# Attention with unsplit exponentials and values: plain fp32 value products on two 64-column halves of the array, and a new queue order

## The chip, the core and the metric

The kernel runs on one core of a Trainium2 chip. The core has five engines with a queue each, which run on their own and wait for one another by semaphores: PE (TensorE, matmuls from SBUF into PSUM), DVE (VectorE), ACT (ScalarE), POOL (GpSimd) and SP (which issues the DMAs). The metric is the time of one execution in microseconds, median of several runs.

## What is computed

Three layers: attention over 2 x 8 heads of 768 tokens with 64 columns, in which a query sees only the keys of its own cluster; a mixture of three linear maps with a maximum and an output map; and eight gated experts. The change is in the first:

```python
q_assign = np.argmax(np.einsum('bhsd,hcd->bhsc', q_n, c_n), axis=-1)
k_assign = np.argmax(np.einsum('bhsd,hcd->bhsc', k_n, c_n), axis=-1)
mask = q_assign[:, :, :, None] == k_assign[:, :, None, :]
scores = scale * np.matmul(q, k.transpose(0, 1, 3, 2))
scores = np.where(mask, scores, -1000000000.0)
scores = scores - np.max(scores, axis=-1, keepdims=True)
attn = np.exp(scores)
attn = attn / (np.sum(attn, axis=-1, keepdims=True) + 1e-09)
return np.matmul(attn, v).astype(np.float32)
```

## The kernel before

All is fp32 in the reference. The kernel mostly multiplies in fp32r, a shorter form of fp32, and splits an operand into a high part (a cast to fp32r) and a low part (the rest), so that a product is a sum of two or three fp32r products.

Attention goes over 96 tiles g, six for each of the 16 heads i; a tile is 128 queries against all 768 keys. `prep` readies a head's keys and queries (POOL, DMA, the cluster masks by `sim`), `prep_v` its values, and `tile_steps` records one tile:

- PE: the scores s, four matmuls of 384 columns (L449, L452). There is one buffer of s.
- DVE: e, the scaled scores with their row minimum (L463). ACT: the exponential of e, in place, with its sum (L471).
- PE: six transposes of e into t (L487), two buffers.
- For two tiles of three: ACT casts t to the high part of at (L232), and DVE subtracts it from t for the low part (L239). For every third tile (`SPARE`): ACT copies t to araw, POOL casts that to the high part (L165) and subtracts for the low part (L239).
- After every second tile, PE: the values y of the pair (L510). v holds 128 columns for each of the six blocks k of keys: 64 of the high part, 64 of the low part. For every k, v is multiplied with the high part and then the low part of at, 256 columns (two tiles), so twelve matmuls add into one y of 128 rows. In which 64 rows the high part of v stands changes from head to head.
- ACT copies one half of y's rows to x32 (L526), then DVE adds the other half (L527).

`prep_v` loads a head's values to natv, and POOL makes the two halves of v (L165, L239).

The order in which the steps stand in the engines' queues is not that of this code. `Plan` records every step with an engine, a cost and what it needs; `order` adds to the urgency of each kind of step a number from the table `MOVES`, makes a schedule by these costs, and the steps are written in that order. Each engine then runs its queue strictly in order. Into this list also go the first steps of the second layer, `weights_first`: three chunks of its weights are turned from 64-bit words into high and low parts (mhi, mlo) by steps of ACT, DVE and POOL on a tile ta (L687 to L701). The program that writes the list begins the matmuls m of the second layer (L707 to L709, by threes) when the last of the scores' exponentials and the third of these chunks are written: from then on it puts three m behind each PE step of attention that is left, up to 18 times.

Of the kernel before, what the change touches and what calls it, by code (L numbers as in the profile page):

```python
# [9 lines left out]
F32R = mybir.dt.float32r  # L10
# [30 lines left out]
class Plan:  # L41
# [19 lines left out]
    def task(self, where, fn, reads=(), writes=(), after=(), due=1e9, shared=False):  # L61

        n = len(self.tasks)
        deps = set(after)
        for s in reads:
            deps.update(s.writers)
        for s in writes:
            if s.before:
                deps.update(s.before.users)
        for s in (*reads, *writes):  # L70
            s.users.append(n)
        for s in writes:
            s.writers.append(n)
        self.tasks.append((*where, fn, deps, due, shared))
        return n
# [62 lines left out]
def moe_kernel(ctx: ExitStack, tc: tile.TileContext, qk, nat, cen, wt, w123, wout, wgate, w1, w2, out):  # L138
    nc = tc.nc
    B, H, S, D = 2, 8, 768, 64  # L140
    C = 16
    P = 128
    NQ = S // P
# [11 lines left out]
    TB = 384  # L155
# [5 lines left out]
    def f32(ap):  # L161
        return ap.bitcast(F32)

    def pool_round(dst, src):
        nc.gpsimd.tensor_scalar(dst, src, 1.0, 1.0, op0=ALU.mult, op1=ALU.mult)  # L165
# [24 lines left out]
    t_p = actx.enter_context(tc.tile_pool(name="t_p", bufs=1, reuse_waits="tile"))  # L190
    d_p = actx.enter_context(tc.tile_pool(name="d_p", bufs=1, space=bass.MemoryType.DRAM, reuse_waits="tile"))
    a_p = actx.enter_context(tc.tile_pool(name="a_p", bufs=1, reuse_waits="tile"))
    ps_a = actx.enter_context(tc.tile_pool(name="ps_a", bufs=1, space=PSUM, reuse_waits="tile"))
    ps_s = sctx.enter_context(tc.tile_pool(name="ps_s", bufs=1, space=PSUM, side="right", reuse_waits="tile"))

    heads = {}
# [7 lines left out]
    plan = Plan()  # L204
# [1 line left out]
    STEP = 2.25  # L206

    MOVES = [
# [6 lines left out]
    ]  # L215
    EARLY = 10.0
    NORM = 2
# [3 lines left out]
    SPARE = lambda g: g % 3 == 2  # L221
    MC_ON = (POOL, 0.83)
    VC_ON = (POOL, 0.51)

    def tile_of(pool, tag, bufs, shape, name, dtype=F32):
        return plan.slot(tag, bufs, lambda: pool.tile(shape, dtype, tag=tag, bufs=bufs, name=name))
# [3 lines left out]
    def copy(engine, dst, src):  # L230
        if engine == ACT:
            nc.scalar.copy(dst, src)  # L232
        elif engine == DVE:
            nc.vector.tensor_copy(dst, src)
        else:
            pool_round(dst, src)

    def sub(engine, dst, a, b):
        (nc.vector if engine == DVE else nc.gpsimd).tensor_sub(dst, a, b)  # L239

    def dma(fn, reads=(), writes=(), after=(), due=1e9, cost=1.0):
        return plan.task((DMA, cost), lambda e: nc.sync.dma_start(*fn()), reads, writes, after, due)
# [160 lines left out]

    def prep_v(i):

        nv = tile_of(a_p, "natv", 1, [P, NQ, D], f"natv{i}")
        v = tile_of(t_p, "v", 2, [P, NQ, P], f"v{i}", F32R)
        half = lambda j: v()[:, :, j * D : (j + 1) * D]
        j = i % 2
        dma(lambda: (nv(), nat[i, :, 2]), writes=[nv])  # L410
        plan.task(VC_ON, lambda e: copy(e, half(j), nv()), [nv], [v])
        plan.task((POOL, 1.0), lambda e: sub(e, half(1 - j), nv(), f32(half(j))), [nv, v], [v])
        heads[i] = *heads[i], v, nv

    def root(n2, y, r, quick=False):

# [19 lines left out]
    def tile_steps(g, st):  # L436

        i = g // NQ
        m, sb, mb, v, nv = heads[i]
        task = plan.task  # L440
        K = D + C
        qs = slice(g % NQ * P, (g % NQ + 1) * P)
        n = slice(g % NQ, g % NQ + 1)
# [32 lines left out]
        gp = g // 2  # L476

        if g % 2 == 0:
            st["at"] = tile_of(t_p, "at", 2, [P, 2, 2, 2, TB], f"at{g}", F32R)
        at = st["at"]  # L480
        t = tile_of(ps_a, "t", 2, [P, 2, 512], f"t{g}")

        def turn():
            for c in range(2):
                for k in range(NQ // 2):
                    ks = slice(k * P, (k + 1) * P)
                    nc.tensor.transpose(t()[:, c, ks], ex()[:, c, ks], ident)  # L487

        hi = lambda: at()[:, 0, g % 2]
        lo = lambda: at()[:, 1, g % 2]  # L490
        turned = lambda: t()[:, :, :TB]
        task((PE, 0.66), lambda e: turn(), [ex], [t])
        if SPARE(g):

            raw = tile_of(a_p, "araw", 1, [P, 2, TB], f"araw{g}")
            task((ACT, 0.8), lambda e: copy(e, raw(), turned()), [t], [raw])
            task((POOL, 0.83), lambda e: copy(e, hi(), raw()), [raw], [at])
            task((POOL, 1.82), lambda e: sub(e, lo(), raw(), f32(hi())), [raw, at], [at])
        else:
            task((ACT, 0.8), lambda e: copy(e, hi(), turned()), [t], [at])  # L500
            task((DVE, 0.95), lambda e: sub(e, lo(), turned(), f32(hi())), [t, at], [at])
        if g % 2 == 0:
            return scored

        y = tile_of(ps_a, "y", 1, [P, 2, P], f"y{gp}")
        m0, o0 = i % 2 * D, (1 - i % 2) * D

        def values(n):
            k, l = n // 2, n % 2
            nc.tensor.matmul(  # L510
                y(), v()[:, k], at()[:, l, :, k // 3, k % 3 * P : (k % 3 + 1) * P], start=n == 0, stop=n == 2 * NQ - 1
            )

        part = []
        for n0 in range(0, 2 * NQ, 3):
            part = [task((PE, 0.352), lambda e, r=range(n0, n0 + 3): [values(n) for n in r], [at, v], [y], part)]
        bi, j, hp = i // H, i % 2, (i % H) // 2
        q0 = (g - 1) % NQ * P
        if j == 0 and q0 == 0:
            st["x"] = [tile_of(a_p, t, n, [P, S], f"{t}_{bi}_{hp}") for t, n in (("x32", 2), ("r32", 1))]  # L520
        x32, r32 = st["x"]

        due = STEP * (g + 1) + DONE
        part_x = lambda: x32()[m0 : m0 + D, q0 : q0 + 2 * P]
        part_y = lambda r0: y()[r0 : r0 + D].rearrange("p a q -> p (a q)")
        task((ACT, 0.37), lambda e: nc.scalar.copy(part_x(), part_y(o0)), [y], [x32], due=due)  # L526
        task((DVE, 0.42), lambda e: nc.vector.tensor_add(part_x(), part_y(m0), part_x()), [y, x32], [x32], due=due)  # L527
        if q0 + 2 * P == S:

            se, rd = (tile_of(a_p, t, 2, [P, NQ], f"{t}{i}") for t in ("se", "rd"))  # L530
# [9 lines left out]
        if j == 1 and q0 + 2 * P == S:  # L540
# [3 lines left out]
            for c in range(2):  # L544
# [6 lines left out]
                    due=due + 20,  # L551
# [7 lines left out]
                    due=due + 20,  # L559
# [323 lines left out]
    for n, (_, i) in enumerate(tasks):  # L883
        engine = plan.tasks[i][0]
# [22 lines left out]
    half = lambda d, h, o, n: [x2[d][:, l, h * HALF + o : h * HALF + o + n] for l in range(2)]  # L907
# [216 lines left out]
    for n in range(len(seq)):  # L1124
        for i in range(2):
# [9 lines left out]
            k = 0  # L1135
# [71 lines left out]
```

## Time and profile before

| | |
|---|---|
| median of 3 runs | 1482.79 us (1482.35 to 1486.88) |
| span of the profiled execution | 1481.2 us |
| PE busy | 1445.4 us, 98% |
| PE weight loads busy | 1246.9 us, 84% |
| DVE busy | 965.9 us, 65% |
| ACT busy | 542.4 us, 37% |
| POOL busy | 703.2 us, 47% |

Busy is the time in which an engine has an instruction under way. A PE matmul's end is modelled and lies behind the start of the next one, so for PE a busy share near 100% doesn't say that no time is lost: the distance from one start to the next does. Attention ends and the second layer's matmuls begin at 277 us of the span.

### The profile page before, as it was taken

The numbers are of one execution on the slowest core, as the hardware profiler recorded it, in microseconds if no ns is written. First come the engines' busy times: TensorE is split into PE (matmuls) and PEld (weight loads), VectorE is DVE, ScalarE is ACT, GpSimd is POOL, SyncE is SP. The second block draws the span as 40 slices with busy tenths as digits, with TensorE's granted clock in tenths as the row PEclk, the third lists the DMA queues.
The fourth block names the chain that finished last, engine by engine and source line by source line (L and its number), as shares of the span: only waits on it lengthen the run. The fifth ranks groups of instructions, "written<-read, shape, count | busy, mean of one in ns | idle before, by whom it ended". The sixth has DMA issues, their size and how long they took to land.

```text
span 1481.2 us, 20488 instructions
## 1 busy us (share of the span) xinstructions
PE 1445.4 (98%) x7718; PEld 1246.9 (84%) x7718; DVE 965.9 (65%) x1687; ACT 542.4 (37%) x1159; POOL 703.2 (47%) x789
## 2 busy tenths in 40 slices
PE   5999998899999999999999999999999999999999
PEld 4999998788887888888888888888888888888887
DVE  5999989745555686765665655656556665566655
ACT  4888888422223522222222222222223222222221
POOL 5899998755754733343333333333333334333330
PEclk9999999999999999999999999999999999999999
DMA  6665531212121100111000110001100011000102
GB/s 176 174 161 131 146 91 47 69 44 71 58 61 45 52 29 29 32 46 37 29 29 29 44 42 29 29 30 43 43 29 29 29 44 43 29 29 29 44 15 86
DMA packets 32292, 83.45 MB, mean 56 GB/s; under 512 B 4576, under 2 KB 10176, under 8 KB 32192
## 3 DMA queue, kind: packets, MB, share of 16 engines
q1 hardware_dynamic: 32192, 82.13, 19.3%
q8 instruction: 61, 1.00, 0.3%
q14 instruction: 39, 0.32, 0.1%
HBM read 65.55 MB, written 3.19 MB: 46 GB/s over the span
## 4 chain that ended last, share of the span: by engine, by line
PE 83%; POOL 7%; DVE 6%; issue 2%; ACT 2%; DMA 0%; POOLq 0%; ACTq 0%; DVEq 0%
PE l L707 12%; PE l L708 11%; PE l L709 11%; PE m L707 3%; PE m L708 3%; PE m L709 3%; PE z L709 3%; PE z L707 3%; PE z L708 3%; PE y L709 3%; PE x L709 3%; PE y L708 3%; PE x L708 3%; PE y L707 3%; PE x L707 3%
## 5 line engine op out<-in xcount | busy, mean ns | idle before, releaser
L1113 DVE SCALAR_TENSOR_TENSOR acc<-l,prob,acc 128x512 f32<-128x512 f32 (+1 forms) x337 | 251.7, 747 | 125.7 <-PE l L709 122.5
L707 PE MATMUL l<-w,h 128*128 128x512 f32 (+1 forms) x770 | 302.5, 393 | 0.0
L708 PE MATMUL l<-w,h 128*128 128x512 f32 (+1 forms) x770 | 301.5, 392 | 0.0
L709 PE MATMUL l<-w,h 128*128 128x512 f32 (+1 forms) x770 | 299.2, 389 | 0.0
L1045 ACT ACTIVATE h<-c 128x512 fp32r<-128x512 f32 (+1 forms) x186 | 97.7, 525 | 368.8 <-DVE c L1074 190.6
L864 POOL TENSOR_TENSOR wop_t<-ts,wop_t 128x256 fp32r<-128x256 f32 x124 | 92.2, 754 | 244.9 <-ACT wop_t L863 244.9
L864 POOL TENSOR_TENSOR wop_b<-wraw,wop_b 128x256 fp32r<-128x256 f32 x97 | 79.6, 821 | 266.0 <-ACT wop_b L863 266.0
L1046 DVE SCALAR_TENSOR_TENSOR h<-c,h 128x512 fp32r<-128x512 f32 (+1 forms) x186 | 112.8, 606 | 110.1 <-ACT h L1045 110.1
L709 PEld LDWEIGHTS l<-w,h 128*128 128x128 f32 x770 | 144.7, 188 | 31.5
L707 PEld LDWEIGHTS l<-w,h 128*128 128x128 f32 x770 | 145.4, 189 | 24.4
L708 PEld LDWEIGHTS l<-w,h 128*128 128x128 f32 x770 | 145.4, 189 | 22.7
L874 POOL TENSOR_TENSOR w<-wraw,w 128x512 fp32r<-128x512 f32 x64 | 83.2, 1301 | 96.3 <-ACT w L873 96.3
L463 DVE TENSOR_SCALAR_CACHE_REDUCE e<-s 128x768 f32<-128x768 f32 x96 | 92.6, 965 | 17.0 <-PE s L452 16.3
L1045 ACT ACTIVATE h<-x 128x512 fp32r<-128x512 f32 (+1 forms) x62 | 30.4, 491 | 188.1 <-PE x L709 188.1
L471 ACT ACTIVATE e<-e,nm 128x768 f32<-128x768 f32 x96 | 90.0, 938 | 16.4 <-DVE e L463 15.9
L510 PE MATMUL y<-at,v 128*128 128x256 f32 x576 | 90.1, 291 | 3.1 <-DVE x L527 2.0
L707 PE MATMUL m<-x,mhi 128*128 128x512 f32 x216 | 84.0, 389 | 0.0
L708 PE MATMUL m<-x,mlo 128*128 128x512 f32 x216 | 84.0, 389 | 0.0
L709 PE MATMUL m<-x,mhi 128*128 128x512 f32 x216 | 84.0, 389 | 0.0
L510 PEld LDWEIGHTS y<-at,v 128*128 128x128 f32 x576 | 78.5, 189 | 6.3 <-POOL at L239 1.8
L709 PE MATMUL x<-x,wop_b 128*128 128x512 f32 (+1 forms) x248 | 83.3, 336 | 0.0
L709 PE MATMUL y<-s,wop_t 128*128 128x512 f32 (+1 forms) x248 | 83.3, 336 | 0.0
(203 smaller groups left out, 3308.1 us busy)
## 6 DMA issues: line engine op xcount, KB each, us to landing
wraw<-in_w SPq DMA_DIRECT2D x64, 512.0 KB
mraw<-in_w SPq DMA_DIRECT2D x18, 512.0 KB
nat<-in_nat SPq DMA_DIRECT2D x16, 384.0 KB
raw<-in_qk SPq DMA_DIRECT2D x16, 384.0 KB
natv<-in_nat SPq DMA_DIRECT2D x16, 192.0 KB
r<-row SPq DMA_DIRECT2D x16, 192.0 KB
mraw<-in_wout SPq DMA_DIRECT2D x8, 384.0 KB
opsb<-opm SPq DMA_DIRECT2D x15, 192.0 KB
```

The lines of the kernel that those rows point to most:

```text
L463: lambda e: nc.vector.tensor_scalar(ex(), scores(), -SCALE, None, op0=ALU.mult, op1=ALU.min, accum_out=nm()),
L471: lambda e: nc.scalar.activation(ex(), ex(), AF.Exp, bias=nm(), scale=-1.0, accum_out=sm()[:, n]),
L510: nc.tensor.matmul(y(), v()[:, k], at()[:, l, :, k // 3, k % 3 * P : (k % 3 + 1) * P], start=n == 0, stop=n == 2 * NQ - 1)
L707: nc.tensor.matmul(ps, whi, xlo, start=first, stop=False, skip_group_check=more)
L708: nc.tensor.matmul(ps, wlo, xhi, start=False, stop=False, skip_group_check=more)
L709: nc.tensor.matmul(ps, whi, xhi, start=False, stop=last, skip_group_check=more)
L864: nc.gpsimd.tensor_sub(w[:, 1], src[key], f32(w[:, 0]))
L874: nc.gpsimd.tensor_sub(w[:, 1], raw[:, j], f32(w[:, 0]))
L1045: nc.scalar.activation(h[:, :, 0], z, AF.Relu)
L1046: nc.vector.scalar_tensor_tensor(h[:, :, 1], z, 0.0, f32(h[:, :, 0]), op0=ALU.max, op1=ALU.subtract)
L1113: nc.vector.scalar_tensor_tensor(a, l2, prob[:, tt, e : e + 1], a, op0=ALU.mult, op1=ALU.add)
```

## The change

The exponentials and the values are no longer split. t is copied as it is into at, by ACT for two tiles of three and by DVE for the third, and at has three buffers for two. The values are loaded straight into v, 64 columns. For every block k there are two matmuls in plain fp32: v against the first tile of the pair into rows 0 to 63 of y, and v against the second tile into rows 64 to 127; the program places them on columns 0 to 63 and 64 to 127 of the array (a split of 128 x 64), twelve for a pair as before, each with 128 columns. ACT copies the first 64 rows of y to x32 and DVE the other 64, neither needing the other. The table of numbers is a new one.

```diff
     MOVES = [
-        0, 177.97, -2.71, 559.73, -10.52, -15.23, 0, 749.02, 2024.58, -254.3, 0,
...
+        -52.63, -92.2, 2849.75, -163.97, -8.36, 9.46, -1.74, 130.75, 119.32, -185.03, -1.09, -99.95, 0, 297.1,
...
     def prep_v(i):
 
-        nv = tile_of(a_p, "natv", 1, [P, NQ, D], f"natv{i}")
-        v = tile_of(t_p, "v", 2, [P, NQ, P], f"v{i}", F32R)
-        half = lambda j: v()[:, :, j * D : (j + 1) * D]
-        j = i % 2
-        dma(lambda: (nv(), nat[i, :, 2]), writes=[nv])
-        plan.task(VC_ON, lambda e: copy(e, half(j), nv()), [nv], [v])
-        plan.task((POOL, 1.0), lambda e: sub(e, half(1 - j), nv(), f32(half(j))), [nv, v], [v])
-        heads[i] = *heads[i], v, nv
+        v = tile_of(t_p, "v", 2, [P, NQ, D], f"v{i}")
+        dma(lambda: (v(), nat[i, :, 2]), writes=[v])
+        heads[i] = *heads[i], v
...
-            st["at"] = tile_of(t_p, "at", 2, [P, 2, 2, 2, TB], f"at{g}", F32R)
+            st["at"] = tile_of(t_p, "at", 3, [P, 2, 2, TB], f"at{g}")
...
-        if SPARE(g):
-
-            raw = tile_of(a_p, "araw", 1, [P, 2, TB], f"araw{g}")
-            task((ACT, 0.8), lambda e: copy(e, raw(), turned()), [t], [raw])
-            task((POOL, 0.83), lambda e: copy(e, hi(), raw()), [raw], [at])
-            task((POOL, 1.82), lambda e: sub(e, lo(), raw(), f32(hi())), [raw, at], [at])
-        else:
-            task((ACT, 0.8), lambda e: copy(e, hi(), turned()), [t], [at])
-            task((DVE, 0.95), lambda e: sub(e, lo(), turned(), f32(hi())), [t, at], [at])
+        evac = (DVE, 0.87) if SPARE(g) else (ACT, 0.8)
+        task(evac, lambda e: copy(e, at()[:, g % 2], t()[:, :, :TB]), [t], [at], shared=SPARE(g))
...
-        y = tile_of(ps_a, "y", 1, [P, 2, P], f"y{gp}")
-        m0, o0 = i % 2 * D, (1 - i % 2) * D
-
-        def values(n):
-            k, l = n // 2, n % 2
-            nc.tensor.matmul(
-                y(), v()[:, k], at()[:, l, :, k // 3, k % 3 * P : (k % 3 + 1) * P], start=n == 0, stop=n == 2 * NQ - 1
-            )
+        y = tile_of(ps_a, "y", 1, [P, P], f"y{gp}")
+        m0 = i % 2 * D
+
+        def values(ks):
+            for k in ks:
+                for l in range(2):
+                    nc.tensor.matmul(
+                        y()[l * D : (l + 1) * D],
+                        v()[:, k],
+                        at()[:, l, k // 3, k % 3 * P : (k % 3 + 1) * P],
+                        start=k == 0,
+                        stop=k == NQ - 1,
+                    )
 
         part = []
-        for n0 in range(0, 2 * NQ, 3):
-            part = [task((PE, 0.352), lambda e, r=range(n0, n0 + 3): [values(n) for n in r], [at, v], [y], part)]
+        for k in range(0, NQ, 2):
+            part = [task((PE, 0.47), lambda e, k=k: values(range(k, k + 2)), [at, v], [y], part)]
...
-        task((ACT, 0.37), lambda e: nc.scalar.copy(part_x(), part_y(o0)), [y], [x32], due=due)
-        task((DVE, 0.42), lambda e: nc.vector.tensor_add(part_x(), part_y(m0), part_x()), [y, x32], [x32], due=due)
+        for l, engine in enumerate((ACT, DVE)):
+            task(
+                (engine, 0.25),
+                lambda e, l=l: copy(e, x32()[m0 : m0 + D, q0 + l * P : q0 + (l + 1) * P], y()[l * D : (l + 1) * D]),
+                [y],
+                [x32],
+                due=due,
+                shared=engine == DVE,
+            )
```

What the new table and the new steps do to the queues, at the places on which the prediction rests. First PE early in attention, where y stands between other matmuls; s are scores, t transposes, y values. Before:

```order
L510 MATMUL y_529<-at_455,v_386 128x256 x3
L487 MATMUL t_533<-ident,e_494 128x128 x6
L449 MATMUL s_547<-opmb_192,opsb_202 128x384 x2
L452 MATMUL s_547<-opm_185 128x384 x2
L510 MATMUL y_529<-at_455,v_386 128x256 x3
L487 MATMUL t_564<-ident,e_524 128x128 x6
L510 MATMUL y_529<-at_455,v_386 128x256 x6
```

After:

```order
L495 MATMUL y_536<-at_403,v_363 64x128 x4
L443 MATMUL s_545<-opmb_189,opsb_191 128x384 x2
L446 MATMUL s_545<-opm_184 128x384 x2
L481 MATMUL t_554<-ident,e_492 128x128 x6
L495 MATMUL y_536<-at_403,v_363 64x128 x4
L481 MATMUL t_572<-ident,e_529 128x128 x6
L443 MATMUL s_583<-opmb_189,opsb_191 128x384 x2
L446 MATMUL s_583<-opm_184 128x384 x2
L495 MATMUL y_536<-at_403,v_363 64x128 x4
```

The twelve y of a pair stand in runs of 3 to 12 before (102 runs in all) and of 4 to 12 after (110 runs).

DVE near the end of attention before, where the steps of the first weight chunk (ta) stand between the scores' passes (e), the subtractions (at) and the sums of y (x):

```order
L463 TENSOR_SCALAR e_3561,nm_3562<-s_3545 128x768
L527 TENSOR_TENSOR x_1_2_3320<-y_3524,x_1_2_3320 64x256
L697 SCALAR_TENSOR_TENSOR ta_1008<-mraw_910,ta_1008 128x512
L463 TENSOR_SCALAR e_3600,nm_3601<-s_3578 128x768
L239 TENSOR_TENSOR at_3603<-t_3569,at_3603 128x768
L239 TENSOR_TENSOR at_3603<-t_3592,at_3603 128x768
L463 TENSOR_SCALAR e_3634,nm_3635<-s_3609 128x768
```

After, the steps of that chunk stand some 220 rows earlier, in the first half of attention:

```order
L683 TENSOR_SCALAR ta_1274<-ta_1274 128x512
L685 SCALAR_TENSOR_TENSOR ta_1274<-mraw_1098,ta_1274 128x512
L457 TENSOR_SCALAR e_1349,nm_1350<-s_1325 128x768
L527 TENSOR_SCALAR se_1362<-sm_1141 128x6
L528 RECIPROCAL rd_1371<-se_1362 128x6
L364 TENSOR_REDUCE sim_1210<-w_1242 128x12
L372 TENSOR_TENSOR oh_1377<-w_1242,sim_1210 128x2x6x16
L457 TENSOR_SCALAR e_1390,nm_1391<-s_1366 128x768
L233 COPY x_0_2_1393<-y_1332 64x128
L233 COPY at_1337<-t_1341 128x768
```

The two chunks behind it, at the very end of attention's list before, are also made in the middle of it now.

PE at the end of attention before:

```order
L487 MATMUL t_3873<-ident,e_3829 128x128 x6
L510 MATMUL y_3880<-at_3802,v_3649 128x256 x12
L535 MATMUL rt_3903<-ident,rd_3890 6x128
L487 MATMUL t_3911<-ident,e_3862 128x128 x6
L510 MATMUL y_3922<-at_3866,v_3649 128x256 x12
L510 MATMUL y_3946<-at_3918,v_3649 128x256 x12
L707 MATMUL m_0_0_3995<-x_98,mhi_1009 128x512
```

After:

```order
L481 MATMUL t_3680<-ident,e_3651 128x128 x6
L495 MATMUL y_3693<-at_3599,v_3521 64x128 x4
L701 MATMUL m_0_0_3698<-x_98,mhi_1275 128x512
L702 MATMUL m_0_0_3698<-x_98,mlo_1276 128x512
L703 MATMUL m_0_0_3698<-x_98,mhi_1275 128x512
L495 MATMUL y_3693<-at_3599,v_3521 64x128 x4
L701 MATMUL m_0_0_3698<-x_99,mhi_1275 128x512
L702 MATMUL m_0_0_3698<-x_99,mlo_1276 128x512
L703 MATMUL m_0_0_3698<-x_99,mhi_1275 128x512
L481 MATMUL t_3713<-ident,e_3676 128x128 x6
```

The last three pairs' y now have m matmuls between them, where before all m stood behind the last y.

## Rows read from the trace of the kernel before

**Rows 1.** Stretches: length, then busy us (instructions) by engine; sum of three attention stretches.

```profile
36.48:221.23 184.75, 178.30 (x1361) 171.25 (x1359) 167.88 (x359) 158.78 (x331) 172.92 (x208) 1.00 0.55 141
221.23:266.02 44.79, 39.21 (x289) 36.33 (x288) 40.90 (x72) 35.45 (x69) 35.64 (x33) 1.00 0.16 45
266.02:277.11 11.09, 8.37 (x62) 7.05 (x61) 8.38 (x14) 7.35 (x14) 6.83 (x5) 1.00 0.19 63
sum 240.63, PE 225.88 PEld 214.63 DVE 217.16 ACT 201.57 POOL 215.39; mean PE 75.29 PEld 71.54 DVE 72.39 ACT 67.19 POOL 71.80
...
296.00:333.00 37.00, 37.00 (x165) 30.66 (x164) 17.79 (x24) 8.42 (x14) 20.02 (x17) 1.00 0.15 43
```

**Rows 2.** Timeline of PE near 230: start, length, operation, instructions of the run.

```profile
227.84 1.47 PE L487 MATMUL t<-ident,e 128*128 128x128 f32 x12
...
229.85 1.60 PE L510 MATMUL y<-at,v 128*128 128x256 f32 x12
231.29 0.51 PE L449 MATMUL s<-opmb,opsb 128*128 128x384 f32 x2
231.64 0.51 PE L452 MATMUL s<-opm 80*128 80x384 f32 x2
```

**Rows 3.** Groups of PE, 36.48 to 277.11: count, busy us, mean ns, idle before.

```profile
L510 PE MATMUL y<-at,v 128*128 128x256 f32 x576 | 90.1, 291 | 3.1 <-DVE x L527 2.0 <-POOL at L239 0.8 <-DVE at L239 0.4
L487 PE MATMUL t<-ident,e 128*128 128x128 f32 x554 | 76.1, 275 | 1.6 <-DVE at L239 0.9 <-ACT e L471 0.6
L449 PE MATMUL s<-opmb,opsb 128*128 128x384 f32 x182 | 51.6, 364 | 10.0 <-DVE e L463 9.9
L452 PE MATMUL s<-opm 80*128 80x384 f32 x182 | 46.8, 338 | 0.0
L314 PE MATMUL sim<-ct,opmb 128*128 128x32 f32 x84 | 11.4, 262 | 0.0
```

**Rows 4.** Waits of PE, 36.48 to 277.11: us in total, times, longest.

```profile
PE s L449 <- DVE e L463: 9.9, 15, 1.5
...
PE y L510 <- DVE x L527: 2.0, 4, 1.1
```

**Rows 5.** Timeline around 243, DVE and PE: a weight step, e, the next scores.

```profile
242.64 2.06 DVE L697 SCALAR_TENSOR_TENSOR ta<-mraw,ta 128x512 f32<-128x512 uint32 x1
...
244.73 0.96 DVE L463 TENSOR_SCALAR_CACHE_REDUCE e<-s 128x768 f32<-128x768 f32 x1
...
245.75 0.62 PE L449 MATMUL s<-opmb,opsb 128*128 128x384 f32 x2 [1.54 <-DVE e L463]
```

**Rows 6.** Timeline of PE at the end of attention.

```profile
266.02 0.51 PE L449 MATMUL s<-opmb,opsb 128*128 128x384 f32 x2
...
274.59 0.35 PE L510 MATMUL y<-at,v 128*128 128x256 f32 x1 [1.06 <-DVE x L527]
275.69 1.58 PE L510 MATMUL y<-at,v 128*128 128x256 f32 x11 [0.75 <-POOL at L239]
```

**Rows 7.** Groups of DVE, POOL and ACT, 36.48 to 277.11, that the change touches.

```profile
L239 POOL TENSOR_TENSOR at<-araw,at 128x768 fp32r<-128x768 f32 x32 | 58.9, 1840 | 2.3
L239 DVE TENSOR_TENSOR at<-t,at 128x768 fp32r<-128x768 f32 x62 | 58.1, 942 | 0.4 <-ACT at L232 0.2
...
L165 POOL TENSOR_SCALAR at<-araw 128x768 fp32r<-128x768 f32 x31 | 25.9, 835 | 9.6 <-ACT araw L232 9.1
L232 ACT COPY araw<-t 128x768 f32<-128x768 f32 x31 | 24.7, 796 | 11.2 <-PE t L487 11.2
...
L527 DVE TENSOR_TENSOR x<-y,x 64x256 f32<-64x256 f32 x47 | 19.7, 420 | 2.4 <-ACT x L526 1.1
...
L526 ACT COPY x<-y 64x256 f32<-64x256 f32 x47 | 17.3, 367 | 9.2 <-PE y L510 8.4
```

**Rows 8.** Plain fp32 matmuls elsewhere (L1018): durations min/median/max in ns; one in the timeline.

```profile
L1018 PE MATMUL cs<-prob,ones x16: 243/274/350, 518.9 to 558.7; 128*128 128x96 f32 x16
...
518.85 0.36 PE L1018 MATMUL cs<-prob,ones 128*128 128x96 f32 x2
```

More of the change, by code (lines that the diff above doesn't have):

```diff
@@ L438, in tile_steps @@
         i = g // NQ
-        m, sb, mb, v, nv = heads[i]
+        m, sb, mb, v = heads[i]
         task = plan.task
@@ L487, in turn @@
                     nc.tensor.transpose(t()[:, c, ks], ex()[:, c, ks], ident)
-        hi = lambda: at()[:, 0, g % 2]
-        lo = lambda: at()[:, 1, g % 2]
-        turned = lambda: t()[:, :, :TB]
         task((PE, 0.66), lambda e: turn(), [ex], [t])
-        if SPARE(g):
-            raw = tile_of(a_p, "araw", 1, [P, 2, TB], f"araw{g}")
-            task((ACT, 0.8), lambda e: copy(e, raw(), turned()), [t], [raw])
-            task((POOL, 0.83), lambda e: copy(e, hi(), raw()), [raw], [at])
-            task((POOL, 1.82), lambda e: sub(e, lo(), raw(), f32(hi())), [raw, at], [at])
-        else:
-            task((ACT, 0.8), lambda e: copy(e, hi(), turned()), [t], [at])
-            task((DVE, 0.95), lambda e: sub(e, lo(), turned(), f32(hi())), [t, at], [at])
+        evac = (DVE, 0.87) if SPARE(g) else (ACT, 0.8)
+        task(evac, lambda e: copy(e, at()[:, g % 2], t()[:, :, :TB]), [t], [at], shared=SPARE(g))
         if g % 2 == 0:
             return scored
-        y = tile_of(ps_a, "y", 1, [P, 2, P], f"y{gp}")
-        m0, o0 = i % 2 * D, (1 - i % 2) * D
-        def values(n):
-            k, l = n // 2, n % 2
-            nc.tensor.matmul(
-                y(), v()[:, k], at()[:, l, :, k // 3, k % 3 * P : (k % 3 + 1) * P], start=n == 0, stop=n == 2 * NQ - 1
-            )
+        y = tile_of(ps_a, "y", 1, [P, P], f"y{gp}")
[10 more added lines that the diff above has]
+                    )
         part = []
-        for n0 in range(0, 2 * NQ, 3):
-            part = [task((PE, 0.352), lambda e, r=range(n0, n0 + 3): [values(n) for n in r], [at, v], [y], part)]
+        for k in range(0, NQ, 2):
+            part = [task((PE, 0.47), lambda e, k=k: values(range(k, k + 2)), [at, v], [y], part)]
         bi, j, hp = i // H, i % 2, (i % H) // 2
@@ L523, in tile_steps @@
         due = STEP * (g + 1) + DONE
-        part_x = lambda: x32()[m0 : m0 + D, q0 : q0 + 2 * P]
-        part_y = lambda r0: y()[r0 : r0 + D].rearrange("p a q -> p (a q)")
-        task((ACT, 0.37), lambda e: nc.scalar.copy(part_x(), part_y(o0)), [y], [x32], due=due)
-        task((DVE, 0.42), lambda e: nc.vector.tensor_add(part_x(), part_y(m0), part_x()), [y, x32], [x32], due=due)
+        for l, engine in enumerate((ACT, DVE)):
[7 more added lines that the diff above has]
+            )
         if q0 + 2 * P == S:
```

9 rows, old and new, of the table MOVES are left out of this document.

## The prediction

> **What bounds the kernel now.** I read the stages first [rows 1]. Their PE column counts a matmul from start to modelled end, so overlapping matmuls fill it and it cannot tell how much room is left; but DVE (91%), POOL (94%) and ACT (86%) are nearly as full as PE in the first stretch, which is all attention. So I took the price of a matmul from starts, not durations [rows 2]: the y run of 12 begins at 229.85 and the next run at 231.29, 1.44 us, or 0.120 each; a run of two s begins 0.35 before the next, 0.175 each; t x12 and four s take 229.85 - 227.84 = 2.01, so a t is (2.01 - 0.70)/12 = 0.109. These runs follow one another t, s, y, s and their times add up, so a change of kind costs next to nothing.
>
> With the counts of the whole stretch [rows 3], y is 576 x 0.120 = 69.1, t 554 x 0.109 = 60.4, s (two lines of 182) 364 x 0.175 = 63.7. The sim matmuls, two lines of 84 of which one stands here, are 18.5 at an estimated 0.11 (the price of t), and some forty little transposes of masks and sums 4. Sum 215.7 of 240.6 us [rows 1]. PE is therefore the bound of attention, and about **25 us of waiting** is all that the other engines can give back. Behind attention PE is busy without a gap (37.00 of 37.00, the last of rows 1), so a microsecond saved before 277 is a microsecond of the end.
>
> What ends PE's waits is mostly DVE's pass over the scores, e (9.9 us, and 2.0 for DVE's sum x [rows 4]): scores have one buffer, and e stands in DVE's queue behind whatever was put before it. One such case: the weight step ta of 2.06 us stands in front of e, and the next scores wait 1.54 [rows 5]. The last wait of all is the tail: from 266.02 to 277.11 PE has 62 matmuls [rows 1], four of them s, 18 t and 36 y (three pairs), 0.70 + 1.96 + 4.32 = 7.0 us of work, so 4 of the 25 us are here; y waits 1.06 for DVE's sum and 0.75 for POOL's part of at [rows 6].
>
> **The change part by part.** *Work taken off DVE, ACT and POOL.* For two thirds of the tiles DVE's subtraction goes (58.1), for one third two POOL passes (58.9 and 25.9) and ACT's plain copy (24.7; the other copies stay as they are, without a cast) [rows 7]. In place of the last DVE gets 32 copies of t; 0.94 as the subtraction of the same tile takes, 30. The two passes over y, of 64 x 256 and one after the other (0.367 then 0.420, 17.3 and 19.7 in all), become two of 64 x 128 side by side, at most as long as before. DVE falls from 217 to 217 - 58 + 30 = 189 us or less of 240.6, ACT from 202 to 177, POOL from 215 to 130, and v needs no POOL at all. DVE's long passes besides e are halved, 64 to 32, which halves what e can stand behind; and the copies of y free it after one pass. So of the 21 us of waits before the tail I expect 13 to go and 8 to stay. Bounds: nothing (each engine in order still keeps e behind something) and all 21.
>
> *The new order.* The three early weight chunks are made in the middle of attention, where before the first was made at its end and two more behind it. That takes the 2.06 us steps off the stretch where they stood alone against e, and it lets the first m matmuls stand between the last y, since m needs only those weights and the first batch's x. Of the 4 us of the tail I take 3. DMA: v lands directly, one load as before; the SP queue keeps its loads, and no row names a DMA among PE's long waits [rows 4]. What PE waits for ahead of 36.48 I leave alone: the same steps stand in the queues there. The wait that is added is that t of every third tile is now freed by DVE, behind e; t has two buffers and DVE is the emptier for it.
>
> *The values on PE.* A plain fp32 matmul is issued as two: eight in the program at L1018 are 16 in the trace [rows 8], and two of them last 0.36 where one lasts 0.274, so the second begins 0.086 after the first; that is for 96 columns, and 0.115 for 128. A pair of tiles has 6 x 2 matmuls, 24 issued. One behind the other they are 24 x 0.115 = 2.76 us against 1.44, and over 48 pairs **+63 us**. If the two halves stream at the same time it is 12 x 0.115 = 1.38, **-3 us**. No row of before shows two matmuls side by side, so both are bounds. I take -2: each half uses its own 64 columns of weights and its own 64 rows of y, its second issue can run with the other half's first, and the array is already seen doing two things at once (weight loads 171 and matmuls 178 us of the same 185 [rows 1]). The Trainium skill, "TensorE: Matmul & The Clock Gate", Part 3, says that matmuls on different column groups run concurrently and gives 2.38x for three; no row here shows it.
>
> *Changing the split of the array.* All matmuls of before use the array whole. In the new order the y stand in 110 runs, between whole-array matmuls, so the array changes 220 times. The kinds of before change for nothing [rows 2]: that is the lower bound. The upper is that each change waits for the last matmul to leave: a y lasts 0.291 [rows 3] and is followed after 0.120, so 0.171, and 220 x 0.171 = 38 us. I take 0.04, near the lower end because that is where a row exists: +9 us. The Trainium skill, "TensorEngine Tiling (Array Packing)", Key Properties, has the rule that speaks against the change: another tiling mode, unlike another tile of the same mode, drains the TensorE. By it the upper bound is the one to take; this trace can neither show nor deny it.
>
> *Sum.* -13 (waits) - 3 (tail) - 2 (values) + 9 (changes) = -9 us. On the profiled execution's span of 1481.2 that is 1472; the median of the runs is 1.6 above that span, so **1474 us**.
>
> **The rivals.** *The halves don't run together* (slower). Place: every y run; price +63; it decides if a half's matmul waits for the other's to have streamed. Then PE is so long that nearly all waits vanish (-20): +43, 1526. A milder form, in which only one of a half's two issues is covered, lies half way: +30 - 20, 1493. For it: a pair needs four weight loads for each k (two halves, two issues) where it needed two, and weight loads already take 171 of 185 us [rows 1]. Against: separate columns, and half as many of them in a load.
>
> *Each change of split drains* (slower, by the other mechanism). 220 x 0.171 = +38, waits -20 (PE again has more slack), values -2, tail included: +16, 1499. It decides from about 0.08 us a change on, where it eats all the gain. For it: y in 110 short runs of 4 to 12 matmuls; against: transposes and matmuls alternate for nothing now.
>
> *The waits stay.* Scores still have one buffer: PE's four s (0.70), then e (0.96 [rows 5]) and again s. With 215 of 240 us used the list is close to its floor; if relief of DVE brings only 4 us and the changes cost 4, the time is 1483 - 2 = 1481: the same.
>
> *All waits go and changes cost nothing*: -25 - 2, 1456. That is the forecast's own better end.
>
> **How the numbers follow.** 0.3% is 4.4 us and about what a measurement can tell from no change. Forecast with its better end, 1456 to 1478: 0.47. Waits stay, 1478 to 1487: 0.16. Drains, or half-covered halves, 1488 to 1505: 0.20. Halves in series, 1505 to 1530: 0.17. So faster 0.47, same 0.16, slower 0.37. The likeliest case alone reaches from 1458 to 1478. The range takes in the better end and the slow cases down to the one with the highest price: 1456 to 1526 leaves out about 0.1 of it.
>
> **What would show it.** Right: y runs of four matmuls (eight issues) that take about 0.47 from start to next start, first t after a y run without a step in starts; the s wait on e below 5 us in all; m matmuls before the last y, so that the first m starts ten or more us ahead of the 277.11 of before. Drains: each y run, or the run behind it, costs 0.1 or more beyond its matmuls, 220 times. Series: runs of four y take 0.9, PE without waits, attention ending near 320. Wrong altogether would be a difference that lies behind attention, where I have put nothing.

## The result

| | before | after |
|---|---|---|
| median of the runs, us | 1483.08 | 1491.7 (1491.25 to 1491.94) |
| ratio to before, 95% interval | | 1.0051 [1.0038, 1.0063] |
| span of the profiled execution, us | 1481.2 | 1489.7 |
| PE busy, us | 1445.4 | 1465.9 |
| DVE / ACT / POOL busy, us | 965.9 / 542.4 / 703.2 | 928.1 / 514.3 / 592.8 |

The changed kernel is slower by 0.5%, 8.6 us, where 1474 us was forecast. The difference lies in attention and the m matmuls right behind it: the last m of the second layer starts at 432.3 us of the span, where it started at 423.8, 8.5 us later, and the spans differ by 8.5 us. 1.5 us of it are a wait of the m for POOL (experiment 8). The first stretch of [rows 1] now reads (length, then busy us and instructions of PE, its weight loads, DVE, ACT, POOL, and the granted clock of PE):

```profile
36.48:221.23 184.75, 182.04 (x1689) 152.23 (x1690) 144.24 (x328) 134.16 (x295) 97.68 (x135) 1.00 0.53 143
```

DVE falls from 168 to 144 of 185 us and POOL from 173 to 98: the relief came as computed. PE is fuller than before, 182 us for 178. Yet a head now takes 15.8 us where it took 14.9 (median distance of every sixth tile's first scores). The groups of PE of [rows 3], 36.48 to 277.11, and its waits of [rows 4]:

```profile
L495 PE MATMUL y<-at,v 128*64 128x128 f32 x1088 | 81.9, 282 | 0.3 <-DVE x L233 0.3
L443 PE MATMUL s<-opmb,opsb 128*128 128x384 f32 x180 | 54.7, 385 | 2.2 <-DVE e L457 2.2
```

```profile
PE s L443 <- DVE e L457: 2.2, 4, 1.0
PE t L481 <- DVE at L233: 0.7, 1, 0.7
PE y L495 <- DVE x L233: 0.3, 1, 0.3
```

The wait of the scores for e went from 9.9 to 2.2 us, and all named waits of PE together from about 15 to about 3.5. PE waits less, is busier, and is slower: the time must be inside its runs. Timeline of PE near 120 (start, length, operation, instructions of the run):

```profile
118.18 0.66 PE L495 MATMUL y<-at,v 128*64 128x128 f32 x8
118.77 0.88 PE L481 MATMUL t<-ident,e 128*128 128x128 f32 x6
...
120.61 0.52 PE L446 MATMUL s<-opm 80*128 80x384 f32 x2
121.06 0.66 PE L495 MATMUL y<-at,v 128*64 128x128 f32 x8
...
122.81 0.51 PE L446 MATMUL s<-opm 80*128 80x384 f32 x2
123.16 0.27 PE L529 MATMUL rt<-ident,rd 128*6 128x128 f32 x1
123.36 1.09 PE L495 MATMUL y<-at,v 128*64 128x128 f32 x16
124.39 0.87 PE L481 MATMUL t<-ident,e 128*128 128x128 f32 x6
125.02 0.48 PE L313 MATMUL sim<-ct,opsb 128*128 128x32 f32 x3
```

Read the distances of starts. Sixteen y take 124.39 - 123.36 = 1.03, eight take 118.77 - 118.18 = 0.59, so eight more cost 0.44: two issues, one in each half, every 0.109 us. The halves do run side by side. But eight at 0.055 each are 0.44 and the run takes 0.59: **0.15 us are lost in every run of y**. Two s ahead of y take 121.06 - 120.61 = 0.45 where the same two ahead of rt take 0.35: another 0.10. And six t behind y take 125.02 - 124.39 = 0.63, where six behind whole-array y take 0.57 (experiment 4). Summed over all 110 runs, the steps ahead of y and inside its runs are 31 us, **0.285 us a run, 0.14 for each change of the split**. What the run behind y loses isn't in this sum, so it is the lower count; experiment 4 gives a fuller one.

### The profile page after: what moved, and what is told of

Read it like the earlier page. It is cut to its first block, busy times and chain, and to the rows that moved or that the text cites. A ratio compares the mean times of both kernels' runs of the same rounds, so it can differ in the third digit from the quotient of the medians.

```text
span 1489.7 us, 21456 instructions
## 1 busy us (share of the span) xinstructions
PE 1465.9 (98%) x8294; PEld 1234.2 (83%) x8294; DVE 928.1 (62%) x1655; ACT 514.3 (35%) x1127; POOL 592.8 (40%) x693
## 4 chain that ended last, share of the span: by engine, by line
PE 94%; DVE 4%; ACT 1%; POOL 1%; issue 1%; DMA 0%; DVEq 0%; ACTq 0%; POOLq 0%
PE l L701 11%; PE l L702 11%; PE l L703 11%; PE y L495 5%; PE t L481 4%; PE m L701 3%; PE z L703 3%; PE z L701 3%; PE z L702 3%; PE m L702 3%; PE m L703 3%; PE s L443 3%; PE y L703 3%; PE x L703 3%; PE y L702 3%; PE x L702 3%
## 5 line engine op out<-in xcount | busy, mean ns | idle before, releaser
L495 PE MATMUL y<-at,v 128*64 128x128 f32 x1152 | 87.2, 282 | 0.3 <-DVE x L233 0.3
L703 PE MATMUL y<-s,wop_t 128*128 128x512 f32 (+1 forms) x248 | 83.3, 336 | 0.0
L702 PE MATMUL y<-s,wop_t 128*128 128x512 f32 (+1 forms) x248 | 83.3, 336 | 0.0
```

Source lines behind the costliest of these rows:

```text
L495: nc.tensor.matmul(y()[l * D : (l + 1) * D], v()[:, k], at()[:, l, k // 3, k % 3 * P : (k % 3 + 1) * P], start=k == 0, stop=k == NQ - 1,)
L702: nc.tensor.matmul(ps, wlo, xhi, start=False, stop=False, skip_group_check=more)
L703: nc.tensor.matmul(ps, whi, xhi, start=False, stop=last, skip_group_check=more)
```

## The experiments

The kernel before measured 1483 to 1485 us beside all of them. Where no interval stands, it is a single run. "Above its pitch" is PE's time from the first s to the first matmul behind the last y, less the settled distance of each of its matmuls times their number: 0.1755 us for an s, 0.109 for a t, 0.112 for a sim, 0.028 for a transpose of a mask or a sum, 0.227 for an m, and for a y 0.120 in fp32r and 0.0545 on the halves.

**1. Fewer runs.** The three parts of a pair's y are held back and written where the last of them stood; all else keeps its order. 48 runs for 110.

```diff
...
-        plan.tasks[i][2](engine)
+        pair, k = parts.get(i, (None, 0))
+        kept_parts.setdefault(pair, []).append(i)
+        if pair is None or k == NQ - 2:
+            for one in kept_parts.pop(pair):
+                plan.tasks[one][2](engine)
```

> The changed kernel with its queue order kept, except that the three parts of a pair's y are brought together at the place of the last one: 48 runs of y instead of 110, nothing else. Theory (each run of y costs 0.28 us beyond its matmuls, because PE stands still when the split of the array changes and again when it changes back): 62 runs less x 0.285 = -17.7, so 1474; up to 1480 if the longer runs let other waits grow. Rival (the runs cost nothing; what was lost lies in waits of the new order): within 2 us of the changed kernel, 1490 to 1494.

Measured 1490.9 us, ratio 1.0050 [1.0033, 1.0067]: no gain. The waits say why (36.48 to 277.11):

```profile
PE s L444 <- DVE e L458: 8.6, 19, 1.0
PE t L482 <- ACT e L466: 1.2, 1, 1.2
```

Four waits for e became nineteen. The likely reading is that the short runs of y had been the work that PE did while DVE made e. So this run doesn't yet tell what a change costs: either the saving was eaten by an order that wasn't made for it, or there was nothing to save.

**2. More runs.** Each part of four matmuls is cut in two, with another PE step between: 176 runs.

```diff
...
-        plan.tasks[i][2](engine)
+        if i in parts:
...
+            fn, k = parts[i]
+            fn(range(k, k + 1))
+            second.append(lambda fn=fn, k=k: fn(range(k + 1, k + 2)))
...
```

> The changed kernel with its order kept, except that the second half of every part of y is put behind the next other step of PE: 176 runs of y instead of 110. Theory (0.285 us a run): 66 x 0.285 = +18.8, so 1510, or down to 1504 where waits of PE take some of it in. Rival (runs cost nothing): 1490 to 1494.

Measured 1522.9 us, ratio 1.0267 [1.0252, 1.0282]: 31 us for 66 runs more, 0.47 each, more than 0.285 and more than both theories allowed. Each run costs, but here y also ends later and with it everything that waits for y, so this is an upper bound.

**3. Which part of the array?** Both tiles of the pair on the first 64 columns, as one matmul of 256 columns for each block of keys; then the same on the second 64.

```diff
-                for l in range(2):
-                    nc.tensor.matmul(
-                        y()[l * D : (l + 1) * D],
-                        v()[:, k],
-                        at()[:, l, k // 3, k % 3 * P : (k % 3 + 1) * P],
-                        start=k == 0,
-                        stop=k == NQ - 1,
-                    )
+                nc.tensor.matmul(
+                    y()[:D],
+                    v()[:, k],
+                    at()[:, :, k // 3, k % 3 * P : (k % 3 + 1) * P],
...
+                    tile_position=(0, 0),
...
```

and for the second half:

```diff
-                    y()[:D],
+                    y()[D:],
...
-                    tile_position=(0, 0),
+                    tile_position=(0, D),
```

> Both tiles of a pair on columns 0 to 63 of the array, one plain fp32 matmul of 256 columns for each block instead of two of 128 side by side; order, runs (110) and all other work as in the changed kernel. Price of the values without halves side by side: 12 issues of some 0.22 against 12 of 0.109, 48 x 1.33 = +64. Theory A (any change to a 64-column split drains): y runs still cost 0.285, time 1492 + 64 less up to 16 us of waits, 1540 to 1556. Theory B (only work on the second column half drains, as the 6-column transposes of the kernel before, which the program places on a split of 32 columns, cost no step): the 31 us go as well, 1509 to 1525, and y begins 0.176 after the last s as the next matmul does elsewhere.

> As the run before, but all values on columns 64 to 127. Theory A (any change of split drains): the same time as that run, 1540 to 1556. Theory B (the second column half drains): some 31 us above that run, 1540 to 1556 with that run at 1509 to 1525.

Measured 1548.8 and 1548.7 us, one run each: no difference. PE in the first of them:

```profile
118.84 1.08 PE L494 MATMUL y<-at,v 128*64 128x256 f32 x4
119.85 0.61 PE L443 MATMUL s<-opmb,opsb 128*128 128x384 f32 x2
...
123.42 1.94 PE L494 MATMUL y<-at,v 128*64 128x256 f32 x8
125.30 0.27 PE L529 MATMUL rt<-ident,rd 128*6 128x128 f32 x1
```

Four take 1.01, eight 1.88: settled 0.87 for four, and the same 0.14 lost in a run. With one half alone the change costs the same, so it isn't the changing from half to half within a run. A pair takes 12 x 0.218 = 2.61 us for 1.31; 48 x 1.30 = 62, of which 57 reached the end. That is what side by side is worth.

**4. The split, or plain fp32?** The values stay plain fp32, but v stands twice in 128 columns and every matmul uses the whole array.

```diff
-        dma(lambda: (v(), nat[i, :, 2]), writes=[v])
+        for j in range(2):
+            dma(lambda j=j: (v()[:, :, j * D : (j + 1) * D], nat[i, :, 2]), writes=[v])
...
-                        y()[l * D : (l + 1) * D],
+                        y()[:, l],
                         v()[:, k],
...
```

> The changed kernel with values in plain fp32 on the whole array: v loaded into both halves of 128 columns, each tile's matmul of 128 columns writes all 128 rows of y, twelve a pair as before, one behind the other. Theory A, it is the split of the array that drains: s to y starts 0.18 us apart again and the run behind a y begins 0.12 us after its last start; a pair's values take 24 issues of 0.11 to 0.12 us, 2.7 to 2.8 us; against the 1549 us of both tiles on one half, 1549 - 31 = 1518 us, up to 8 more for waits that come back. Theory B, it is plain fp32 among fp32r matmuls that drains, whatever the columns: s to y stays at 0.26 to 0.27 us and the step behind a run stays, and the time is about 1549 us.

Measured 1535.3 us. The pitches decide, not the time:

```profile
117.78 0.61 PE L496 MATMUL y<-at,v 128*128 128x128 f32 x4
118.23 0.82 PE L482 MATMUL t<-ident,e 128*128 128x128 f32 x6
118.80 0.60 PE L444 MATMUL s<-opmb,opsb 128*128 128x384 f32 x2
119.24 0.52 PE L447 MATMUL s<-opm 80*128 80x384 f32 x2
119.59 1.06 PE L496 MATMUL y<-at,v 128*128 128x128 f32 x8
120.48 0.82 PE L482 MATMUL t<-ident,e 128*128 128x128 f32 x6
```

Four issues take 0.45, eight 0.89, the two s ahead 0.35: no step anywhere. Over the whole trace s to y is 175 ns in the median (267 in the changed kernel), y to t 112 (203). **It is the split of the array that costs, not the type.** The same triples also give the full price. Two s, eight y, two s take 0.446 + 0.588 + 0.455 us in the changed kernel and 0.355 + 0.807 + 0.433 here (medians from start to start of the next run); less the y at their pitch, 0.436 and 0.896, that is 0.35 us more a run. Six t, eight y, six t in the same way give 0.33. So a change costs 0.17 us and the 110 runs 36 to 39, against 31 by the lower count. The time is 17 above the 1518 expected: 24 issues of 0.112 are 2.69 us a pair, 4 us more than the one half's in all, and the rest are waits, some of them of t for the exponential (3.0 us).

**5. The change without the split.** The changed order, copies and relief, with the value matmuls of before: fp32r, whole array.

```diff
...
-                        y()[l * D : (l + 1) * D],
+                        y(),
                         v()[:, k],
-                        at()[:, l, k // 3, k % 3 * P : (k % 3 + 1) * P],
+                        at()[:, :, k // 3, k % 3 * P : (k % 3 + 1) * P],
...
```

> The changed kernel with its order, its copies of t and y and its relief of DVE, POOL and ACT, but with the value matmuls of before: twelve fp32r matmuls a pair of 256 columns, on the whole array (the high part of at taken twice, and v rounded and put by POOL into both halves of its 128 columns, so the values come out rounded and doubled). 106 runs of y. Theory, drains are what took the gain: the 0.138 us before and 0.149 us behind each run go (-31 us), a pair's values take 1.44 us for 1.31 (+6), some of the waits come back (0 to +10): 1466 to 1476 us, that is faster than before as I had forecast. Rival, the chain of scores, e and the new list set the pace and the drains only fill time in which PE would have waited: waits come back by 20 us or more, 1486 to 1492 us.

PE in it, near 126:

```profile
125.66 0.52 PE L453 MATMUL s<-opm 80*128 80x384 f32 x2
126.02 0.64 PE L502 MATMUL y<-at,v 128*128 128x256 f32 x4
126.49 0.71 PE L488 MATMUL t<-ident,e 128*128 128x128 f32 x5
```

Four y take 0.47, the two s ahead of them 0.36: no step. Measured 1479.5 us, ratio 0.9967 [0.9954, 0.9979]; span 1477.9. Between the two theories. The split and its steps cost 12 us of span (1489.7 - 1477.9), although at least 31 us of steps go and only 6 come back in longer values: 13 us or more returned as waiting. Above its pitch PE loses 34.1 us here and 35.7 before (262.4 us of attention with 36 m in it, 255.8 with none); the changed kernel lost 50.7 (271.3 with 30 m), of which 31 to 39 are the steps and 12 to 20 waits. So the steps had stood in the place of waits, as I suspected of experiment 1. Not all of it can be named: the gaps of PE of over 0.1 us from the first s on sum to 17.7 us before, 6.4 in the changed kernel and 12.2 here; the rest lies under the modelled ends of matmuls. And the whole of the relief with the new order is worth 3.3 us of span (3 to 7 by the interval of the times), not 16; 2.2 of them lie where I had put nothing, ahead of the first s, which starts at 19.2 us for 21.4.

**6. The relief alone.** The kernel before with its order, less the 64 subtractions of DVE (62 of them between 36.48 and 277.11) and the POOL passes over at; y takes the high part of at twice. First with DVE copying every third t, as the change has it; then with ACT still copying all of them.

```diff
-            task((ACT, 0.8), lambda e: copy(e, raw(), turned()), [t], [raw])
-            task((POOL, 0.83), lambda e: copy(e, hi(), raw()), [raw], [at])
-            task((POOL, 1.82), lambda e: sub(e, lo(), raw(), f32(hi())), [raw, at], [at])
+            task((ACT, 0.8), lambda e: copy(DVE, hi(), turned()), [t], [raw])
+            task((POOL, 0.83), lambda e: None, [raw], [at])
+            task((POOL, 1.82), lambda e: None, [raw, at], [at])
...
-            task((DVE, 0.95), lambda e: sub(e, lo(), turned(), f32(hi())), [t, at], [at])
+            task((DVE, 0.95), lambda e: None, [t, at], [at])
...
```

and for the second:

```diff
-            task((ACT, 0.8), lambda e: copy(DVE, hi(), turned()), [t], [raw])
+            task((ACT, 0.8), lambda e: copy(e, hi(), turned()), [t], [raw])
```

> The kernel before, with its order, its y and its fp32r matmuls on the whole array, but without the work that the change takes off: no subtraction on DVE, no POOL passes, and for every third tile DVE copies t in place of ACT and POOL (the high part of at is taken twice, so the low part's product is wrong). It tells what relief of DVE and POOL is worth without the new order. By my forecast it is 13 us of PE's waits: 1468 to 1474 us. Rival, seen in the changed order on the whole array (1479 us): scores have one buffer and each engine keeps its order, so most waits stay: 1477 to 1482 us.

> As the run with relief alone, but ACT still makes the copy of every third tile (straight into at), so that DVE gets nothing new: 62 subtractions of 0.94 us and all POOL passes over at are gone, every queue and PE's order are otherwise those of before. In the run with DVE's copies they stood in front of the mask step oh and the masks' transposes waited 13 us; those waits must go. By my forecast's step (relief takes 13 us of PE's waits): 1468 to 1474 us. Rival, the waits for e come from the one buffer of scores and from where e stands in a fixed order, not from how full DVE is: 1477 to 1483 us.

Measured 1494.3 us, 1.0068 [1.0054, 1.0082], and 1485.5 us, 1.0009 [1.0000, 1.0019]. Less work made the kernel slower, or at best changed nothing. The first, in ten of the heads, 13.4 us in all (DVE, then PE):

```profile
115.65 0.96 DVE L234 CAST at<-t 128x768 fp32r<-128x768 f32 x1 [1.83 <-PE y L510]
...
116.91 0.80 DVE L373 TENSOR_TENSOR oh<-w,sim 128x192 bf16<-128x192 f32 x1
...
117.76 0.31 PE L385 MATMUL ot<-ident,oh 128*96 128x128 bf16 x2 [1.50 <-DVE oh L373]
```

DVE's new copy waits 1.83 us for a y (the y reads the buffer of at that the copy is to write); the mask step oh stands behind it, and PE's next instruction wants oh. In the second, DVE has 160 us of work in 241 (36 to 277) where it had 218. PE's waits (20 to 279), and one case:

```profile
PE t L487 <- ACT e L471: 9.5, 11, 1.1
PE s L449 <- DVE e L463: 8.5, 16, 1.5
```

```profile
111.36 0.79 ACT L232 CAST at<-t 128x768 fp32r<-128x768 f32 x1
111.45 0.96 DVE L463 TENSOR_SCALAR_CACHE_REDUCE e<-s 128x768 f32<-128x768 f32 x1 [0.73 <-PE s L452]
...
114.31 0.80 ACT L232 CAST at<-t 128x768 fp32r<-128x768 f32 x1 [2.16 <-PE y L510]
...
115.00 0.94 ACT L471 ACTIVATE e<-e,nm 128x768 f32<-128x768 f32 x1
...
116.08 0.88 PE L487 MATMUL t<-ident,e 128*128 128x128 f32 x6 [1.10 <-ACT e L471]
```

The waits for e fell from 12.1 to 8.5 us (20 to 279). But ACT's next copy of t waits 2.16 us for y to free its at; e is done at 112.4, its exponential stands behind that copy until 115.0, and PE's t waits 1.10: 11 times, 9.5 us. Taken off one queue, the wait moved to another.

**7. The old work in the new order.** The changed kernel, with DVE's subtraction and the two POOL passes put back as work that nothing needs.

```diff
...
+            if SPARE(g):
+                pool_round(scratch, at()[:, g % 2])
+                nc.gpsimd.tensor_sub(scratch, at()[:, g % 2], scratch)
+            else:
+                nc.vector.tensor_sub(scratch, t()[:, :, :TB], at()[:, g % 2])
...
```

> The changed kernel with the work that it took off DVE and POOL put back as work that nothing needs: behind each ACT copy of t a DVE subtraction of 128 x 768 into a scratch tile, behind each DVE copy of t two POOL passes of 128 x 768; same order, same PE work. It tells what the relief is worth. Theory, relief of DVE is what took 16 us of PE's waits away: they come back, +10 to +17 us, 1501 to 1508 us, with PE's waits for e near 10 us again. Rival, the waits fell because the drains make PE longer (and because of the new list) and DVE has time in any case: within 3 us of the changed kernel, 1490 to 1494 us.

Measured 1551.0 us, ratio 1.0450 [1.0434, 1.0465]: 59 us more than the changed kernel, over three times the 17 that I had thought at most. PE's waits, 36.48 to 277.11, which here is only the first three quarters of attention, and the stretch from 20 to 277 in the order of [rows 1]:

```profile
PE s L443 <- DVE e L457: 21.9, 33, 2.2
PE y L505 <- DVE x L233: 4.7, 7, 1.9
PE ot L384 <- DVE oh L372: 4.0, 4, 2.1
...
20.00:277.00 257.00, 216.56 (x1769) 177.67 (x1769) 205.16 (x402) 146.66 (x317) 167.86 (x193) 0.94 0.41 115
```

Not all of the 59 us is waiting. In this stretch, in which PE waits this often, its granted clock is 0.94 in the mean, between its levels of 1.2 and 2.4 GHz, where the changed kernel has 1.00; at most that costs 0.06 x 257 = 15 us, an estimate. The subtraction of DVE also reads t, so t is free only when DVE is done. With 6 this still shows that relief has no price of its own: the passes are worth nothing in the order that was made with them, and at least some 44 us in the order that was made without.

**8. The tail.** All m behind the last y, as before.

```diff
-    DRAIN = 18
+    DRAIN = 0
```

> The changed kernel with all m matmuls of the second layer behind the last y, as before; the weights are still made early. It tells what the m between the last y are worth, for which I had put 3 us. Theory, they fill the waits of the tail: without them the tail's waits return (+3 to +4 us) and some seven runs of y join others (-2 us): 1491 to 1494 us. Rival, they fill nothing and only add changes of split: 1487 to 1490 us.

Measured 1490.2 us, ratio 1.0044 [1.0026, 1.0062], against 1.0051 [1.0038, 1.0063]: the m between the last y are worth nothing, at best. In the changed kernel, then in this run, without m between:

```profile
277.40 0.66 PE L495 MATMUL y<-at,v 128*64 128x128 f32 x8
277.99 0.50 PE L701 MATMUL m<-x,mhi 128*128 128x512 f32 x1
...
297.77 0.50 PE L701 MATMUL m<-x,mhi 128*128 128x512 f32 x1 [1.50 <-POOL x L238]
```

```profile
280.51 1.53 PE L495 MATMUL y<-at,v 128*64 128x128 f32 x24 [0.69 <-DVE x L233]
282.73 1.53 PE L495 MATMUL y<-at,v 128*64 128x128 f32 x24 [0.69 <-DVE x L233]
284.19 0.50 PE L701 MATMUL m<-x,mhi 128*128 128x512 f32 x1
```

They fill two waits of 0.69, but make seven more runs of y (7 x 0.285 = 2.0), and an m later waits 1.50 for POOL's x, which it has caught up with.

**9. An order that knows what a change costs.** If the steps are real and experiment 1 only lacked an order, then an order made for it should win. The planner charges PE 0.14 us where y and another kind meet, a further number (KEEP) makes it stay with the kind at hand, and the table of numbers is made anew (47 and 46 runs of y); no m between the last y.

```diff
...
+            turn = self.CHANGE if e == PE and split[i] != last else 0.0
+            return max(ready[i], free[e] + turn, port if self.port[i] else 0.0)
...
+            i = min((i for i in queue[e] if start(i, e) <= t + patience), key=lambda i: (urgency[i] + (self.KEEP if e == PE and split[i] != last else 0.0), i))
...
```

> The changed kernel with another order: the planner that makes the order is told that PE loses 0.14 us wherever y follows another kind or another kind follows y, and its table of numbers is made anew for that; all m stand behind the last y. The twelve y of a pair then stand together, 47 runs for 110, as in the run with the parts gathered, but with the other engines' queues made for it. Theory, the gathered parts gained nothing because the rest of the order was made for short runs: some 62 runs fewer save 62 x 0.285 = 17.7 us, of which up to 8 are lost in waits: 1474 to 1482 us, level with or a little faster than before. Rival, with one buffer of scores whatever is saved in changes comes back as waits for e: 1487 to 1492 us.

> As the run before it, with a second table of numbers made in the same way (46 runs of y). It tells how far the result depends on the one table: by the theory 1474 to 1484 us, by the rival 1487 to 1492 us.

Measured 1470.0 us, ratio **0.9902 [0.9888, 0.9915]**, and 1479.8 us, 0.9969 [0.9956, 0.9981]. Both beat the kernel before, the first by 1%; it is 21.7 us below the changed kernel with the same arithmetic. Its y and its waits for e (36.48 to 277.11):

```profile
123.66 1.53 PE L501 MATMUL y<-at,v 128*64 128x128 f32 x24
125.12 0.62 PE L449 MATMUL s<-opmb,opsb 128*128 128x384 f32 x2
```

```profile
PE y L501 <- DVE x L239: 0.7, 1, 0.7
PE t L487 <- DVE at L239: 0.5, 1, 0.5
PE t L487 <- ACT e L471: 0.4, 1, 0.4
PE s L449 <- DVE e L463: 0.3, 1, 0.3
```

Twenty-four issues take 1.46: 12 x 0.109 and one step of 0.15. With 63 runs fewer, 63 x 0.285 = 18 us are saved by the lower count, and this time they stay saved: above its pitch PE loses 30.9 us, where experiment 8, whose m also stand behind the last y, loses 51.5. The second table loses 35.8. The two differ by 9.8 us, about half of what the runs save; 3.7 of it lies ahead of the first s (19.0 and 22.7 us), where the second has a wait of 4.3 us for a DMA. No table was made anew for the kernel before or for experiment 5, so how much of the gain over the kernel before is the charge and how much the new search isn't separated.

## Why the prediction was wrong

The sum was -13 (waits) - 3 (tail) - 2 (values) + 9 (changes) = -9; the spans differ by +8.5. The step that failed is the price of a change of the split.

- **The bound was read rightly**: PE in attention, with nothing behind it. Prices from starts and not from durations were what made the step of 0.15 us visible.
- **Values, -2**: right in kind, -6 in size. A pair takes 1.31 us for 1.44; the issues of the two halves start 7 ns apart. The Trainium skill, "TensorE: Matmul & The Clock Gate", Part 3, says that column groups run concurrently; this trace agrees, with 2.61 us on one half against 1.31 on two.
- **Changes, +9**: the step that failed first. I took 0.04 us a change, near the row in which kinds followed each other for nothing, though those rows held no change of this split; measured is 0.14 by the lower count and 0.17 by the fuller one, at the upper bound of 0.171, so 31 to 39 us for the 9. The bound was right and the choice between its ends wrong: a row of another mechanism is no nearer for being at hand. The Trainium skill, "TensorEngine Tiling (Array Packing)", Key Properties, says that changing the tiling mode drains the TensorE. Experiment 4 agrees, with 175 ns from s to y on the whole array and 267 into the split.
- "All matmuls of before use the array whole" was also untrue: rt uses 6 columns. I took it that the program places it on a split of 128 x 32, which no view here shows; before, y to rt is 116 ns and rt to y 26, no step. If it is such a split, not every change costs, and why that one is free stays open.
- **Waits, -13, and tail, -3**: failed as well, though the waits shrank as if it had held. In the changed kernel PE loses 12 to 20 us beside the steps, where before it lost 36 in all, so with 31 for the changes and -6 for the values the sum would come to +9, next to the +8.5. That is luck: most of the waits went because steps stood in their place. Without the split nearly all of them are back (34 us above the pitch), and relief and order together give 3.3 us of span (experiment 5). I had let work taken off DVE free e in proportion. With fixed queues it gave nothing in the old order (experiment 6) and little in the new one (5); what the other engines may be given depends on the order (7). The tail's 3 us were worth nothing (8).
- **The terms don't add.** Steps and waits on one engine fill the same time: 31 - 6 us or more of work added on PE moved the end by 12. The rival "each change of split drains" had just this form, with steps at 38, waits at -20 and values at -2: 1499, 7 above the 1492 measured, of which 4 are the values. In kind it was the true case, and it shared its 0.20 of the chance with half-covered halves.
- **What would show it** did not tell the cases apart. The sign of the drains came, 0.1 us or more a run, and so did the step behind a y run that "right" ruled out (0.59 for eight issues, not 0.47). But two signs of "right" came too: the s wait on e below 5 us (2.2), and m ahead of the last y. The first m, forecast ten us earlier, came at 276.5, 0.6 earlier.

Not settled: why the step is 0.15 in the run and 0.10 ahead of it; whether the array empties at a change or the weight load merely comes late, since the traces show the step and not its inside; and how much of the 9.8 us between the two tables is chance.

## What to carry to other kernels

Count how often a kernel changes the split of the PE array, and price each change at the cost of a drained array (0.14 to 0.17 us here), not at that of ordinary alternation; then group the split work, and give the price to whatever makes the order. Relief of an engine that is off the bound is worth what a new order can make of it: in a fixed order it may be nothing or less. Don't add a saving of waits to a cost on the same engine as if they were independent. When a first cure (fewer changes) brings nothing, look at the waits before dropping the theory: the time may have moved there, and an order made for the cure may bring it back.

## What the hardware showed that I had not expected

- A run of matmuls on 64 columns between whole-array matmuls cost 0.285 us by the lower count and 0.33 to 0.35 by the fuller one, about the same on either half and with both; plain fp32 on the whole array cost no step (s to y 175 ns for 267).
- Two plain fp32 matmuls on the two halves start 7 ns apart and a pair of issues of 128 columns takes 0.109 us, the price of one on the whole array (0.112).
- Weight loads of y are not made ahead over the change: in the changed kernel they wait on nothing that the profile shows, 71 times, and those of t 35 times (36.48 to 277.11). In the kernel before, the last line, it was 3 times.

```profile
PEld y L495 <- issue: 15.5, 71, 0.3
PEld t L481 <- issue: 6.0, 35, 0.2
...
PEld y L510 <- issue: 1.1, 3, 0.7
```
